# Output blocks summed in accumulating DMA stores, masks by affine selects on GpSimd, and another order

## The chip, the cores and the metric

The kernel runs on one core of a Trainium2 chip. The metric is the device time of one execution in microseconds; the time before is the median of three runs. Engines are called as in the profile: PE (matrix multiplication), DVE (VectorE), ACT (ScalarE), POOL (GpSimd) and SP (SyncE, which here only issues DMAs). Each engine works through its own queue in order; semaphores hold an instruction back until its inputs are there, and everything behind it on that engine waits too.

## What is computed

Causal attention over 8 batches of 8 heads, 576 tokens and 64 columns a head, with 16 further "beacon" keys that every token sees, and behind it a feed-forward layer with an elu between two multiplications (512 to 2048 to 512 columns) on all 4608 tokens.

```python
scores = scale * np.matmul(q, k_all.transpose(0, 1, 3, 2))   # k_all: beacon_k, then k
scores = np.where(causal, -1000000000.0, scores)             # beacons are never masked
a = np.exp(scores - scores.max(-1, keepdims=True))
a /= a.sum(-1, keepdims=True) + 1e-09
x = np.matmul(a, v_all)                    # then (tokens, heads * 64)
h = x @ w_in
g = np.where(h > 0.0, h, np.exp(np.minimum(h, 0.0)) - 1.0)
out = g @ w_out                            # 4608 x 512, float32
```

## The kernel before

The order of all work is written out by hand: one long string of words (L800 to L915) such as `S.3.0` or `J.1.4`, each a step (a function with its arguments) that issues a few instructions. The scheduler keeps that order, so each engine's queue is the string filtered by engine. Letters are steps, the first number a batch (attention) or a tile of tokens (feed-forward).

**Loads.** `lq` (L136), `lv` (L144, L149), `wi` (L160) and `wo` (L163) load queries and keys of the first three batches, values, and the two weight matrices, all by DMAs that POOL issues. From batch 3 on, `lk` (L769) copies q or k of a batch to a scratch in DRAM as bf16, also from POOL, and `lt` (L776) brings it back transposed with DMA transposes issued by SP: `lt.b.0` serves head pairs 0 and 1 (tile qst for one parity of batches), `lt.b.1` pairs 2 and 3. `lp` (L785, L786) puts the beacon keys beside them with small POOL operations.

**Attention.** `T`, `cq`, `ck` transpose q and k of the first batches on PE and drain them. `S` (L318) multiplies scores into one of two PSUM buffers of tag S, `x` (L333, ACT) takes the exponential into the tile et; batches from 1 on have 13 such groups of 512 columns over four head pairs. `m` zeroes what causality forbids by multiplying with triu on DVE (L338): `m.b.p.0` does key blocks 0 and 1 of two head pairs in one operation of 128x1024, `m.b.p.1` blocks 2 and 3 in one and block 4 (80 rows) in another. `D` (L396) adds key blocks on DVE, `L` (L376, L422) sums on PE, `n` (ACT) takes the reciprocal by Ln and Exp, `W` (L376) multiplies by the values, `M` (L474) scales into xT.

**Feed-forward.** Ten tiles of tokens: 0 and 1 have 256, the others 512. `F` (L514) multiplies by w_in, `e` (L524, ACT) takes the exponential, the relu is `u` (L530 on ACT, or with `.v` L532 on DVE) and `k` (L544) makes elu of both on DVE; or `r` (L551) and `g` (L556) make it on DVE without a relu. The last two tiles use a Strassen form with steps X, P, K, E, U (with `.v` on DVE, L737) and V. The second multiplication is in Strassen-Winograd form for all tiles from 1 on (tile 1 takes tile 0 with it): `wt` and `Z` (L566, DVE) make sums of weights and of g, `Q` (L618, PE) runs seven products of 16 matmuls each (words count matmuls, `Q.1.0.7` is the first seven), in PSUM of tag ops with two buffers.

**Output.** After product ph, `J.t.ph` drains it. For ph 0, 2 and 3 the bank is copied to the tile sm on ACT, or on DVE with `.v` (L628). For ph 1, 4 and 5 DVE adds the bank and an sm tile into osb (L635), ph 6 is a copy to osb (L633), and SP stores the 256 KB of osb into its block of the output (L639). sm and osb have three buffers each. The last tile ends with half copies, `Jh`. PE's first words, `wm` and `warm`, are matmuls on zeros.

Of the kernel before, what the change touches and what calls it, by code (L numbers as in the profile page):

```python
# [17 lines left out]
def kernel(  # L18
# [325 lines left out]
    def m(b, p, g):  # L344

        if b > 0:
            t = et4(b, p)
# [273 lines left out]

    @step
    def J(t, ph, eng="s"):

        if ph in (0, 2, 3):
            sm[t, ph] = melt.tile([P, 2, HM], FP32, tag="sm", name="sm")
            for q_, y in both(xy[t, PH[ph][0]]):
                (nc.scalar.copy if eng == "s" else nc.vector.tensor_copy)(out=sm[t, ph][:, q_, :], in_=y)  # L628
# [171 lines left out]
    wm.4 wm.4 warm.4 wm.4 lq.0.0.0.4 lq.0.1.0.4 wm.4 warm.4 ident lq.0.0.4.8 wm.4 T.0.1.0 bt  # L800
    warm.4 lq.0.1.4.8 bk cb.0.3 T.0.0.0 cb.0.1 cb.0.0 ck.0.1.0 S.0.1.0 ck.0.0.0 T.0.1.1 x.0.1.0
    S.0.0.0 x.0.0.0 T.0.0.1 cq.0.1.1 S.0.1.2 cq.0.0.1 T.0.3.0 S.0.0.2 x.0.1.2 T.0.2.0 x.0.0.2
    cq.0.3.0 S.0.0.3 cb.0.2 lq.1.0.0.4 S.0.3.0 T.0.3.1 cq.0.2.0 x.0.0.3 lv.0.0.1 cq.0.3.1
    x.0.3.0 T.0.2.1 S.0.0.1 tri wm.4 x.0.0.1 S.0.3.2 x.0.3.2 S.0.1.3 cq.0.2.1 x.0.1.3 wm.4 wm.4
    S.0.2.0 wm.4 wm.4 x.0.2.0 S.0.3.3 wm.4 x.0.3.3 S.0.2.3 x.0.2.3 wm.4 m.0.3.0 S.0.3.1 cb.1.0
    x.0.3.1 lv.0.2 m.0.1.0 m.0.2.0 m.0.0.0 L.0.A m.0.1.2 n.0.A m.0.0.2 T.1.0.0 wi.2 m.0.3.2
    cq.1.0.0 S.0.2.1 W.0.A.1 x.0.2.1 W.0.A.0 S.0.1.1 x.0.1.1 T.1.1.0 M.0.A.1 S.0.2.2 M.0.A.0
    x.0.2.2 F.0.5 cq.1.1.0 e.0.5 lv.0.3.4 m.0.2.2 wi.1 m.0.0.3 m.0.1.3 S.1.5 S.1.1 x.1.5 m.0.3.3
    F.0.4 x.1.1 lq.1.0.4.8 wi.0 m.0.2.3 L.0.B cb.1.1 e.0.4 W.0.B.1 n.0.B S.1.3 cb.1.3 u.0.4.v
    M.0.B.1 u.0.5.v F.0.2 x.1.3 e.0.2 r.0.2 S.1.4 x.1.4 S.1.0 x.1.0 F.0.3 T.1.3.0 ck.1.3.0  # L810
    W.0.B.0 g.0.2 wi.3 k.0.4 S.1.12 m.1.0.0 k.0.5 M.0.B.0 e.0.3 F.0.1 x.1.12 T.1.2.0 S.1.10
    r.0.3 g.0.3 F.1.0 cq.1.2.0 cb.1.2 e.0.1 u.0.1 x.1.10 k.0.1 F.1.1 e.1.0 S.1.8 lq.2.0.0.4
    u.1.1.v u.1.0 k.1.0 x.1.8 F.0.0 e.1.1 S.1.9 S.1.6 u.0.0.v lq.2.0.4.8 F.0.6 k.1.1 x.1.9
    lp.3.1 e.0.0 T.2.1.0 F.1.3 x.1.6 u.0.6.v e.0.6 cq.2.1.0 S.1.11 cb.2.0 lv.1.0.1 e.1.3 x.1.11
    S.1.7 k.0.0 F.0.7 S.1.2 u.1.3.v F.1.5 x.1.7 x.1.2 T.2.0.0 k.0.6 lv.1.2.3.4 u.0.7.v e.0.7
    m.1.1.1 T.2.2.0 ck.2.0.0 u.1.5.v ck.2.2.0 m.1.1.0 wo.1 e.1.5 m.1.0.1 F.1.6 wo.3 k.0.7 L.1.1
    L.1.0 wo.0 F.1.2 e.1.6 wo.2 k.1.5 lk.3.0 u.1.6.v lk.3.1 F.1.4 cb.2.1 cb.2.2 n.1.1 M.1.1.0
    W.1.0 k.1.6 n.1.0 M.1.0.0 u.1.2 W.1.1 lv.2.2.3.4 u.1.4 M.1.0.1 lk.4.0 e.1.2 lv.3.2.3.4 k.1.3
    S.2.4 e.1.4 x.2.4 F.1.7 M.1.1.1 k.1.4 u.1.7 e.1.7 F.2.13 T.2.3.0 S.2.8 u.2.13 k.1.7 F.2.12
    e.2.13 x.2.8 F.2.9 u.2.12 cq.2.3.0 S.2.3 e.2.12 k.2.13 S.2.1 e.2.9 wt.1.0 k.1.2 x.2.3 F.2.2  # L820
    e.2.2 lv.2.0.1 Z.1.3.B Q.1.0.7 x.2.1 Q.1.7.14 u.2.9.v S.2.2 S.2.0 u.2.2 k.2.12 F.2.6 k.2.9
    Q.1.14.21 x.2.0 x.2.2 F.2.15 cb.2.3 wt.1.1 e.2.6 wt.2.1 u.2.6 u.2.15 Q.1.21.28 e.2.15
    m.2.0.0 S.2.6 S.2.5 wt.2.0 F.2.4 J.1.0 x.2.5 F.2.10 Z.1.1.B Z.1.2.B S.2.11 x.2.6 Q.1.28.35
# [121 lines left out]
```

## Time and profile before

| | |
|---|---|
| median of 3 runs | 330.53 us (330.32 to 330.69) |
| the profiled execution's own time | 329.86 us |
| its span, first to last instruction | 328.2 us |
| granted TensorE clock | 1.0 |
| DMA | 34.65 MB, mean 106 GB/s |
| POOL-issued queue, SP- and ACT-issued queue | 18.49 MB, 15.34 MB |

The profile is of one execution. Its page gives the busy time of each engine, the span in 40 equal slices (a digit is the busy share in tenths), and groups of instructions by line: source line, engine, operation, output and input tiles with shapes, count, then busy time, mean duration in ns, and the idle time of the engine just before them with what ended it. Stretch rows give the busy time of each engine in a part of the span; a timeline lists merged instructions with start and duration. Issues of DMAs have a size and the time from issue to landing.

### The profile page before, as it was taken

Reading aid. Unit: us, or ns where it says so; the run is one execution under the profiler, and the core shown is the slowest. Engines: PE = TensorE matmul, PEld = TensorE weight load, DVE = VectorE, ACT = ScalarE, POOL = GpSimd, SP = SyncE. Lnnn points to the kernel's source line nnn. Section 1 sums busy time; section 2 is a strip of 40 time slices with the busy share of each in tenths; the row PEclk is TensorE's granted clock in tenths of the full one; section 3 lists DMA queues with packets and bytes.
Section 4 is the critical chain, followed back from the end, with each engine's and each line's share of the span. In section 5 each row is a group of like instructions: output and inputs, shape, how many; then the busy total and the mean of one; then the engine's idle time right before and its main releaser. Section 6 shows DMA issues by size and latency. Waiting matters only on the chain.

```text
span 328.2 us, 8827 instructions
## 1 busy us (share of the span) xinstructions
PE 318.5 (97%) x3648; PEld 215.7 (66%) x3648; DVE 296.9 (90%) x527; ACT 276.4 (84%) x449; POOL 85.2 (26%) x109
## 2 busy tenths in 40 slices
PE   7879999999999999999999999999999999999995
PEld 4656766566555655566555665566665888888884
DVE  2677998999998999999989989999999999999992
ACT  2979999998889897999999888988699598889930
POOL 8973791742705626004010500000000000000000
PEclk9999999999999999999999999999999999999999
DMA  9999999999999999995922792010110021111113
GB/s 115 169 190 206 172 167 185 151 151 154 174 173 154 136 172 151 188 116 61 160 82 58 77 106 84 12 34 2 66 34 33 2 96 34 34 65 34 35 64 128
DMA packets 130520, 34.65 MB, mean 106 GB/s; under 512 B 112816, under 2 KB 130480, under 8 KB 130480
## 3 DMA queue, kind: packets, MB, share of 16 engines
q0 software_dynamic: 95840, 18.49, 69.1%
q1 hardware_dynamic: 33920, 15.34, 23.8%
q8 instruction: 28, 0.46, 0.6%
q10 hardware_dynamic: 720, 0.26, 0.3%
q14 instruction: 12, 0.10, 0.1%
HBM read 37.22 MB, written 15.34 MB: 160 GB/s over the span
## 4 chain that ended last, share of the span: by engine, by line
PE 72%; DMA 12%; ACT 7%; POOL 4%; DVE 3%; issue 2%; DVEq 0%; POOLq 0%
PE ops L618 27%; PE hps L514 22%; DMA v<-in_v_dram 10%; PE hps L706 8%; PE sc L318 5%; ACT et L333 5%; PE ut L376 5%; PE sx L618 2%; POOL scr L769 1%; POOL v L149 1%; DMA kst<-in_k_dram 1%; ACT e L524 1%; POOL w_out L163 1%; DVE qkp L396 1%; PE lt L422 1%
## 5 line engine op out<-in xcount | busy, mean ns | idle before, releaser
L333 ACT ACTIVATE et<-sc 128x1024 f16<-128x1024 f32 (+2 forms) x114 | 104.2, 968 | 8.1 <-PE sc L318 7.6
L514 PE MATMUL hps<-xT,w_in 128*128 128x512 f16 (+1 forms) x512 | 110.7, 353 | 0.3 <-DVE gt L556 0.3
L618 PEld LDWEIGHTS <-gt 128*128 128x128 f16 x864 | 83.0, 98 | 21.1 <-issue 2.9
L524 ACT ACTIVATE e<-hps 128x512 f32<-128x512 f32 x112 | 66.7, 615 | 9.0 <-PE hps L514 4.1
L514 PEld LDWEIGHTS <-w_in 128*128 128x128 f16 x512 | 46.8, 98 | 39.0 <-issue 5.5
L544 DVE SCALAR_TENSOR_TENSOR gt<-e,r 128x512 f16<-128x512 f32 x103 | 68.6, 683 | 2.2 <-ACT e L524 0.7
L618 PE MATMUL ops<-w_out,gt 128*128 128x256 f16 x416 | 54.7, 273 | 0.0
L618 PE MATMUL ops<-wt,gt 128*128 128x256 f16 x400 | 53.6, 273 | 0.0
L530 ACT ACTIVATE r<-hps 128x512 f16<-128x512 f32 x74 | 45.0, 616 | 4.5 <-PE hps L514 4.3
L149 POOL DMA_DIRECT2D v<-in_v_dram x40 | 36.4, 1016 | 3.5 <-DMA v<-in_v_dram 1.9
L566 DVE TENSOR_TENSOR gt<-gt 128x2048 f16<-128x2048 f16 (+1 forms) x30 | 33.1, 1110 | 0.1
L338 DVE TENSOR_TENSOR et<-et,triu 128x1024 f16<-128x1024 f16 (+4 forms) x66 | 26.6, 447 | 1.8 <-ACT et L333 1.7
L532 DVE TENSOR_SCALAR r<-hps 128x512 f16<-128x512 f32 x29 | 19.9, 685 | 4.0 <-ACT e L524 3.2
L376 PEld LDWEIGHTS <-v 128*32 128x32 f16 (+1 forms) x800 | 17.2, 96 | 9.4 <-issue 1.2
L745 DVE SCALAR_TENSOR_TENSOR gt<-e,r 128x512 f16<-128x512 f32 x32 | 21.5, 683 | 0.5 <-ACT kst L716 0.4
L376 PE MATMUL ut<-et,v 128*32 128x464 f16 (+3 forms) x560 | 21.1, 296 | 0.3 <-DMA v<-in_v_dram 0.3
L396 DVE TENSOR_TENSOR qkp<-qkp,et 128x1344 f16<-128x1344 f16 (+2 forms) x33 | 19.2, 583 | 0.4
L635 DVE TENSOR_TENSOR osb<-ops,sm 128x512 f32<-128x512 f32 x26 | 17.7, 682 | 1.3 <-PE ops L618 1.3
L716 ACT COPY kst<-hps 128x512 f32<-128x512 f32 x24 | 13.9, 589 | 4.8 <-PE hps L706 4.6
L474 DVE TENSOR_TENSOR xT<-ut,rl 128x672 f16<-128x672 f32 (+12 forms) x26 | 16.4, 669 | 0.7 <-PE ut L376 0.4
L618 PE MATMUL ops<-w_out,s 128*128 128x256 f16 x128 | 16.9, 273 | 0.0
L618 PEld LDWEIGHTS <-s 128*128 128x128 f16 x144 | 13.9, 98 | 2.5
(118 smaller groups left out, 415.7 us busy)
## 6 DMA issues: line engine op xcount, KB each, us to landing
out_dram<-osb SPq DMA_DIRECT2D x35, 256.0 KB, 2.2
v<-in_v_dram POOLq DMA_DIRECT2D x24, 128.0 KB, 11.8
scr<-in_q_dram POOLq DMA_DIRECT2D x5, 576.0 KB, 16.2
scr<-in_k_dram POOLq DMA_DIRECT2D x5, 576.0 KB, 18.1
w_in<-in_moe_w_in_dram POOLq DMA_DIRECT2D x8, 256.0 KB, 8.7
w_out<-in_moe_w_out_dram POOLq DMA_DIRECT2D x4, 512.0 KB, 10.5
qst<-in_q_dram POOLq DMA_DIRECT2D x4, 288.0 KB, 9.6
kst<-in_k_dram POOLq DMA_DIRECT2D x4, 288.0 KB, 10.0
```

The lines of the kernel that those rows point to most:

```text
L149: nc.gpsimd.dma_start(out=vt[b][r0:r0 + n, j, :, :], in_=v[b, :, ilo[j]:ilo[j] + n, :].rearrange("h s d -> s h d"),)
L333: nc.scalar.activation(out=ets[b, d][:, :, a - EC2 * d:e - EC2 * d], in_=sc[b, g][:, :, a - c0:e - c0], func=AFT.Exp, bias=0.0, scale=SCALE)
L338: nc.vector.tensor_tensor(out=o, in0=o, in1=i, op=ALU.mult)
L376: nc.tensor.matmul(out=t[32 * i:32 * (i + 1), a - qa:e - qa], lhsT=ones[0:kc[j], :] if half is None else v16[0:kc[j], j, h, half:D:2], rhs ...
L396: nc.vector.tensor_tensor(out=o, in0=t[0:rows, :, a:e] if n == 0 else o, in1=t[0:rows, :, col:col + e - a], op=ALU.add)
L514: nc.tensor.matmul(out=h[:, n_, :], lhsT=w_in16[:, cc, P * fc:P * (fc + 1)], rhs=xt[k][:, cc, a - TT * k:e - TT * k], start=(cc == 0), sto ...
L524: nc.scalar.activation(out=eb[t, i], in_=flat(hp[t, i]), func=AFT.Exp, bias=0.0, scale=1.0)
L530: nc.scalar.activation(out=rb[t, i], in_=flat(hp[t, i]), func=AFT.Relu, bias=0.0, scale=1.0)
L544: nc.vector.scalar_tensor_tensor(out=half(t, i), in0=eb[t, i], scalar=1.0, in1=rb[t, i], op0=ALU.subtract, op1=ALU.min)
L566: (nc.vector if eng == "v" else nc.gpsimd).tensor_tensor(out=o_, in0=a_, in1=b_, op=op_)
L618: nc.tensor.matmul(out=half_of(xy[t, n_], qd), lhsT=lw[:, P * qd:P * (qd + 1)], rhs=wt_[:, c, :], start=(first and c == 0 and (qd == 0 or ...
L706: nc.tensor.matmul(out=hx[t, g, n_][:, c, :], lhsT=lw, rhs=rh, start=(first and c == 0 and k_ == 0), stop=(k_ == 1), skip_group_check=True)
```

## The change

Three things. First, for all tiles but the last (TA = 9), DVE no longer adds the two parts of an output block. The first part (ph 0, 3 or 2) is stored to its output block from sm by SP as soon as it is drained, the second part (ph 1, 4 or 5) is copied from PSUM to osb by ACT or DVE, and POOL issues a DMA that adds osb to the block in DRAM. Second, 20 of the 40 mask steps go from DVE to POOL (words that end in `.p`): each key block is cut by one affine_select of its own, in place. Third, the whole string is in another order, and some relus, J copies and elu forms are on the other of ACT and DVE. The set of steps is otherwise the same: 1430 words in both.

```diff
+    def cut(o, base):
+        nc.gpsimd.affine_select(
+            out=o, in_=o, compare_op=ALU.is_ge, fill=0.0, base=base, channel_multiplier=-1,
+            pattern=[[0, o.shape[1]], [1, o.shape[2]]])
...
-    def m(b, p, g):
+    def m(b, p, g, eng="v"):
...
+            if eng == "p":
+                for j in (0, 1) if g == 0 else (2, 3, 4):
+                    c, w = lays[b][j][3], min(P, lays[b][j][2] - lays[b][j][1])
+                    cut(t[0:kc[j], :, c:c + w], NB if j == 0 else 0)
+                return
...
+    TA = len(tiles) - 1
+
+    def block(t, ph):
+        i, m_ = {1: (0, 0), 4: (1, 1), 5: (0, 1), 6: (1, 0)}[ph]
+        row = (tiles[t][0] if t > 1 else 0) + 256 * i
+        return out[row:row + 256, HM * m_:HM * (m_ + 1)].rearrange("(q p) m -> p q m", p=P)
...
+            if t < TA:
+                nc.sync.dma_start(out=block(t, {0: 1, 3: 4, 2: 5}[ph]), in_=sm[t, ph])
             return
...
-            if ph == 6:
+            if ph == 6 or t < TA:
...
+        if ph == 6 or t >= TA:
+            nc.sync.dma_start(out=block(t, ph), in_=osb)
+        else:
+            nc.gpsimd.dma_start(out=block(t, ph), in_=osb, accum_op=ALU.add)
```

The queues of POOL and SP that follow from the two strings, from batch 1's values on:

```
POOL before: lq.2.0.4.8 lp.3.1 lv.1.0.1 lv.1.2.3.4 wo.1 wo.3 wo.0 wo.2 lk.3.0 lk.3.1 lv.2.2.3.4
  lk.4.0 lv.3.2.3.4 lv.2.0.1 lp.3.0 lk.4.1 lk.5.1 lk.5.0 lv.3.0.1 lk.6.0 lp.4.1 lp.4.0 lp.5.1 lk.6.1
POOL after:  lq.2.0.0.4 m.1.0.0.p lq.2.0.4.8 lv.1.2.3.4 lv.1.0.1 wo.1 m.1.1.1.p m.1.0.1.p wo.0 wo.2
  wo.3 lp.3.0 lk.3.0 lk.3.1 lv.2.0.1 lk.4.0 lv.2.2.3.4 lk.4.1 m.2.0.0.p J.1.1.v lv.3.2.3.4 lp.4.1
  lp.3.1 lv.3.0.1 m.2.1.0.p J.1.4.v lk.6.1 lp.4.0 J.1.5.v lk.5.0 lk.5.1 m.3.0.0.p lk.6.0 lp.5.0 J.2.1.v
SP before:   lt.3.0 lt.3.1 J.1.1 J.1.4 J.1.5 lt.4.0 J.1.6.v lt.4.1 lt.5.0 J.2.1 lt.5.1 J.2.4
SP after:    lt.3.0 J.1.0.v lt.3.1 J.1.2.v J.1.3 lt.4.0 lt.4.1 J.1.6.v J.2.0.v J.2.2.v lt.5.0 J.2.3
```

More of the change, by code (lines that the diff above doesn't have):

```diff
@@ L799 @@
     run("""
[L800 to L823, printed above, removed]
```

219 lines of the change are left out of this document (122 added, 97 removed).

## The prediction

> **What bounds the kernel now.** I read the busy times first, then the same times by stretch, then the PE's rows with the idle time before each, then the queues that feed PE.
>
> ```profile
> PE 318.5 (97%) x3648; PEld 215.7 (66%) x3648; DVE 296.9 (90%) x527; ACT 276.4 (84%) x449; POOL 85.2 (26%) x109
> ...
> DMA  9999999999999999995922792010110021111113
> ```
> ```profile
> 0.00:10.00 10.00, 8.02 (x96) 4.87 (x96) 3.31 (x13) 3.60 (x5) 8.81 (x18) 1.00 1.05 123
> 10.00:20.00 10.00, 9.31 (x228) 6.66 (x232) 7.27 (x23) 9.93 (x15) 8.84 (x14) 1.00 1.59 176
> 20.00:40.00 20.00, 17.96 (x332) 12.93 (x325) 16.21 (x35) 18.11 (x25) 10.52 (x16) 1.00 1.40 193
> 40.00:60.00 20.00, 19.85 (x348) 12.77 (x346) 18.14 (x34) 19.39 (x32) 10.93 (x12) 1.00 1.69 172
> 60.00:80.00 20.00, 19.96 (x168) 12.37 (x167) 19.72 (x30) 18.78 (x29) 11.43 (x11) 1.00 1.96 149
> 80.00:100.00 20.00, 19.64 (x259) 11.63 (x258) 18.77 (x34) 16.99 (x27) 6.66 (x8) 1.00 2.18 167
> 100.00:120.00 20.00, 19.47 (x200) 11.56 (x197) 18.33 (x30) 18.60 (x28) 10.06 (x11) 1.00 1.75 153
> ...
> 220.00:240.00 20.00, 20.00 (x197) 12.70 (x199) 19.09 (x33) 14.77 (x25) 0.00 (x0) 1.00 0.08 28
> ...
> 320.00:328.20 8.20, 4.58 (x42) 3.84 (x40) 1.97 (x4) 0.37 (x1) 0.00 (x0) 1.00 0.38 128
> ```
>
> The columns of the second fence are the stretch and its length, then PE, PEld, DVE, ACT and POOL, granted clock, DMA share, GB/s. PE is the bound. It is idle 328.2 - 318.5 = 9.7 us in all: 1.98 in the first ten microseconds, 0.69 in the next ten, 2.04 up to 40, 3.62 behind 320 (the last matmul, copy and store), and so only some 1.4 between 40 and 320. From 220 to 240 the idle time is zero although DVE works 19.1 of 20 there. DVE at 90% is thus no second bound: what is taken off it can give back at most those 1.4 us, plus what little it holds up in the start. The second thing to see is that the DMA engines are full until 147 us (the digits are 9 for 18 slices of 8.2 us). Where PE does wait in that time, it waits for a load:
>
> ```profile
> 60.01 1.69 PE L618 MATMUL ops<-w_out,gt 128*128 128x256 f16 x14
> ...
> 78.69 0.63 PE L318 MATMUL sc<-qst 64*128 64x512 bf16 x8
> ...
> 83.00 1.31 PE L376 MATMUL ut<-et,v 128*32 128x464 f16 x36 [0.26 <-DMA v<-in_v_dram]
> ...
> 86.41 0.61 PE L318 MATMUL sc<-kst 64*128 64x272 bf16 x8
> ...
> 104.67 0.61 PE L318 MATMUL sc<-qst 64*128 64x64 bf16 x6 [0.27 <-POOL qst L786]
> ```
>
> So loads arrive just in time at 83.0, and at 104.67 too: the POOL row named there was a write for another batch, and the last thing that batch 4's scores need is its transposed load, which SP issues from 90.7 on. The kernel stands on a full PE fed by a full DMA queue with almost no margin at two places. That is what this change touches.
>
> **The change, part by part.** First the exchange between DVE and ACT.
>
> ```profile
> L544 DVE SCALAR_TENSOR_TENSOR gt<-e,r 128x512 f16<-128x512 f32 x103 | 68.6, 683 | 2.2 <-ACT e L524 0.7 <-PE ops L618 0.7 <-ACT r L530 0.4
> ...
> L532 DVE TENSOR_SCALAR r<-hps 128x512 f16<-128x512 f32 x29 | 19.9, 685 | 4.0 <-ACT e L524 3.2 <-PE hps L514 0.3
> L338 DVE TENSOR_TENSOR et<-et,triu 128x1024 f16<-128x1024 f16 x28 | 18.9, 682 | 0.6 <-ACT et L333 0.5
> L635 DVE TENSOR_TENSOR osb<-ops,sm 128x512 f32<-128x512 f32 x26 | 17.7, 682 | 1.3 <-PE ops L618 1.3
> ...
> L556 DVE TENSOR_TENSOR gt<-hps,r 128x512 f16<-128x512 f32 x9 | 6.2, 691 | 0.3
> L628 DVE COPY sm<-ops 128x512 f32<-128x512 f32 x7 | 4.8, 681 | 0.0
> ...
> L551 DVE TENSOR_SCALAR r<-e 128x512 f16<-128x512 f32 x9 | 4.5, 497 | 1.5 <-ACT e L524 1.5
> L338 DVE TENSOR_TENSOR et<-et,triu 80x320 f16<-80x320 f16 x14 | 4.4, 315 | 0.0
> ...
> L737 DVE TENSOR_SCALAR r<-kst 128x512 f16<-128x512 f32 x3 | 1.3, 421 | 0.0
> ```
>
> An addition (L635) costs DVE 682 ns and the copy that takes its place 681 (L628), so a block left on DVE saves nothing; only those that go to ACT do. By the order's words DVE has 24 J steps in place of 37: 13 x 0.682 = 8.9 us off. Masks: 12 steps with one 128x1024 operation (batch 0's one, which is smaller, counted so) and 8 with a 128x1024 and an 80x320 one, 12 x 0.682 + 8 x 0.997 = 16.2 off. Added: 10 more relus of a tile (L532), 6.9, and 7 of the last two tiles (L737), 2.9. Three elu blocks change from the r,g form to the k form: 3 x (0.683 - 0.497 - 0.691) = -1.5. DVE: -16.8 us. ACT takes 13 copies and gives 14 relus: about nothing. PE's work is the same, matmul for matmul. With the 1.4 us of the first part, I put this relief at -0.5 (0 to -1.4).
>
> Next the masks on POOL and what stands behind them.
>
> ```profile
> L238 POOL TENSOR_SCALAR_AFFINE_SELECT triu<-triu 128x256 f16<-128x256 f16 x1 | 0.4, 402 | 0.0
> ...
> L238 POOL TENSOR_SCALAR_AFFINE_SELECT triu<-triu 128x128 f16<-128x128 f16 x1 | 0.3, 287 | 0.1
> ```
> ```profile
> 40.05 3.02 POOL L163 DMA_DIRECT2D w_out<-in_moe_w_out_dram  x4
> 43.00 2.31 POOL L769 DMA_DIRECT2D scr<-in_q_dram  x1
> ```
> ```profile
> 42.59 2.85 ACT L333 ACTIVATE et<-sc 128x1024 f16<-128x1024 f32 x3
> ```
> ```profile
> 59.27 6.10 SPq L776 DMA_TRANSPOSE qst<-scr  x2
> 65.48 7.61 SPq L776 DMA_TRANSPOSE kst<-scr  x2
> ```
>
> From 256 and 128 columns, 0.9 ns a column: a cut of 4x128 is estimated at 0.63 us, one of 4x80 at 0.46. The 20 masks are 49 cuts, about 28.7 us of POOL, which has room (85 of 328). It is their place that costs. In the new order two masks of batch 1 stand in POOL's queue ahead of three of the four w_out loads and of batch 3's scratch copies. The second needs x.1.2, the last of the three ACT operations that end at 45.4. Before, POOL issued these loads from 40 to 47 waiting for nobody. Now the mask runs 45.4 to 47.2 at best, 49 if it waits for its turn beside DVE, and the loads behind it go 6 to 8 us later. Three w_out pieces of 512 KB at the stretch's 172 GB/s are 3.0 us each, so the last lands at 56 to 59, and the first reader on PE is at 60.0: just covered. The two scratch copies land by the same rate some 7 us later, at 64 to 67 in place of 59.3 (where SP's transposes begin). SP then needs 6.1 and 7.6 us for them, and the second pair now has tile 1's first output store ahead of it. Their readers on PE are at 78.7 and 86.4; before, with 9.2 us from an issue to its landing (row below), the first pair was down by 62.3 + 9.2 = 71.5 and the second by some 78.5, 7 and 8 us ahead of them. That margin is used up. I take 1.0 us for this, between 0 and 4.
>
> The third part is the traffic of the accumulating stores.
>
> ```profile
> out_dram<-osb SPq DMA_DIRECT2D x2, 256.0 KB, 7.7
> ```
> ```profile
> out_dram<-osb SPq DMA_DIRECT2D x35, 256.0 KB, 2.2
> ...
> qst<-scr SPq DMA_TRANSPOSE x10, 9.2
> ```
>
> The first row is from 115 to 123 us: a store lands 7.7 us after its issue while the loads run, 2.2 over the whole kernel. Each of eight tiles now has three more transfers, 24 x 256 KB, and three of its seven read the output back to add. Tiles 1 and 2 and the start of 3 fall in the full stretch: 14 more transfers by 150 us, 6 of them by 105. At 153 to 172 GB/s 256 KB are 1.5 to 1.7 us; an accumulating one isn't shown by any row, so between the same and twice that. Six are 9 to 15 us of DMA time, less if stores fill gaps of the small packets, ahead of the load that PE met with 0.27 us of waiting at 104.67. Against it: SP's new order puts batch 4's transposes ahead of J.1.5's and J.1.6's stores, where they stood behind J.1.5 and so started at 90.7. That gives back up to about 10 us. Also, POOL's accumulating stores wait in their queue for the first store to land, and behind J.1.1 stand batch 3's values and the beacon columns, behind J.1.5 batch 5's copies. I take 1.0 us, between 0 and 6. Behind that stretch I let the same transfers cost nothing: the digits fall to 0 to 2 with a few loads between, POOL has little else to do, and a store lands in 2.2 again.
>
> Then the lock, where the trace shows one side only:
>
> ```profile
> 130.29 0.72 POOL L786 COPY qst<-bkT 128x32 bf16<-128x32 bf16 x1
> ...
> 143.66 0.21 POOL L786 COPY qst<-bkT 128x32 bf16<-128x32 bf16 x1 [12.65 <-PE sc L318]
> ```
> ```profile
> 130.26 0.93 DVE L338 TENSOR_TENSOR et<-et,triu 128x1024 f16<-128x1024 f16 x2
> ...
> 143.62 0.68 DVE L635 TENSOR_TENSOR osb<-ops,sm 128x512 f32<-128x512 f32 x1
> ```
>
> The same small POOL copy takes 0.21 beside a DVE operation that reads PSUM and SBUF, and 0.72 beside one that reads SBUF twice: it ends only when the first mask has. So a cut on POOL will wait for DVE's k, Z, D and mask operations, 0.5 us or so each time. Whether DVE also waits for a cut, no row shows, since POOL's copies are too short. The loss on DVE is between nothing and 28.7 us, the whole time of the cuts; if two thirds of DVE's time are such operations (an estimate: k in L544 alone is 68.6 of 296.9, and Z, D and the masks come on top), about 19. The relief is 16.8, so DVE ends between 280 and 309, and I count 0.5 us for PE (0 to 5), near the middle where both cancel.
>
> The Trainium skill, SBUF — State Buffer, section "Who interferes with whom", says that a DVE instruction with two SBUF inputs and a GpSimd instruction that reads SBUF exclude each other, and that the second one waits for all of the first. The trace agrees for the POOL side (0.21 against 0.72); by that rule the DVE side is the 19 us above.
>
> The start: the warm-up matmuls are as many, and 16 score blocks pass through ACT, which is busy 9.93 of 10 us from 10 to 20, in either order. 0, with 1.5 either way. The tail is the same copies and stores: 0.
>
> Sum: -0.5 + 1.0 + 1.0 + 0.5 + 0 = +2.0 us on the profiled execution's 329.86 (span 328.2 and 1.66 around it), 331.9; the median of the runs lies 0.67 above that execution, so 332.5. The case by itself spans 331.3 to 335.
>
> **Rivals.** (1) Faster: PE's holes close. The waits at 83.0 (batch 2's values now go ahead of batch 3's), 104.67 and those of the start, 4.7 us up to 40, shrink, and a DVE with 17 us less work holds nobody up. For it: these waits are real, and SP's order does let batch 4's load go earlier. Against it: most of the start waits for first loads and for ACT, which the change doesn't shorten. Price -0.7 to -2.5; at -1.3, 329.2. It decides if the scratch copies of batch 3 land before 64 us and no two-input DVE operation is longer than its 0.68. (2) Everything is absorbed: 330.5, within 0.2%, about what a measurement of this kernel can tell from no change. For it: 8 us of margin on the transposes, and no PE idle at all after 120. (3) The lock bites: DVE waits for nearly every cut, D and k come late, PSUM banks are not freed, and PE stalls from 90 to 235 us, where the masks are. Of the 19 to 29 us that DVE loses, what goes beyond the 16.8 taken off it, 2 to 12, reaches PE by half: 1 to 6, with the late loads' 2 it is +3 to +8, 336. For it: the 0.72 row and a DVE at 19.7 of 20. Against: the 16.8 us taken off DVE. (4) POOL's queue blocks so hard (each wait of an accumulating store delays loads behind it) that a batch's loads are late by more than 5 us: over 337.
>
> **How the numbers follow.** Forecast 0.40 (332.5), rival 1 0.27, rival 2 0.13, rival 3 0.14, rival 4 0.06. Faster by over 0.2% (0.66 us): 0.27. Within: 0.13. Slower: 0.40 + 0.14 + 0.06 = 0.60. The range leaves out rival 4 and the far end of rival 1 and of rival 3: 329.0 to 337.5.
>
> **What would show it.** Right: PE idle of 1 to 3 us between 55 and 130, before sc<-qst, sc<-kst, ut or ops rows, with a DMA as releaser; w_out issued after 47; SP's first transposes after 64; stores in the full stretch landing after more than 7 us. Lock: L544, L566 and L396 rows above their 683 to 1220 ns while POOL cuts, and cuts of 1 us and more. Wrong: PE idle before 40 us below 4.7 and none between 40 and 130 (rival 1), or PE waiting for DVE after 150 us, where I see no cost at all.

## The result: 343.6 us, 4% slower

The changed kernel takes 343.60 us (343.27 to 345.92), the kernel before 330.42 us on the same chip: a ratio of 1.0415, 95% interval 1.0367 to 1.0462. That is 13.2 us more, where I forecast 2.0, and far beyond the range's end at 337.5. The profiled execution took 343.88 us with a span of 342.2.

Page of the changed kernel, busy times and DMA slices:

```profile
PE 321.4 (94%) x3647; PEld 216.9 (63%) x3648; DVE 296.2 (87%) x498; ACT 277.3 (81%) x448; POOL 152.9 (45%) x182
...
DMA  9999979999999999999991328913213352352362
```

Two things are to be seen. DVE is as busy as before (296.2 against 296.9), although by the words of the order 16.8 us of work went from it. And PE is idle for 342.2 - 321.4 = 20.8 us in place of 9.7, and 2.9 us longer busy with the same matmuls; together 14.0, the growth of the span. The same stretches as before show where (length, PE, PEld, DVE, ACT, POOL, granted clock, DMA share, GB/s):

```profile
20.00:40.00 20.00, 17.75 (x354) 13.03 (x342) 14.83 (x32) 16.86 (x23) 11.23 (x17) 1.00 1.31 186
40.00:60.00 20.00, 18.60 (x341) 12.55 (x338) 18.44 (x31) 18.16 (x29) 14.57 (x18) 1.00 1.21 141
60.00:80.00 20.00, 19.61 (x164) 11.69 (x163) 19.94 (x28) 18.90 (x31) 10.33 (x9) 1.00 2.05 164
80.00:100.00 20.00, 20.00 (x262) 12.18 (x260) 18.80 (x35) 17.48 (x26) 13.00 (x20) 1.00 1.91 169
100.00:120.00 20.00, 15.25 (x126) 8.50 (x123) 13.41 (x17) 15.19 (x22) 14.38 (x18) 1.00 1.98 177
120.00:140.00 20.00, 16.26 (x196) 8.96 (x197) 15.91 (x26) 13.90 (x23) 8.08 (x9) 0.83 2.08 157
```

From 40 to 60 PE is idle for 1.40 us (before 0.15), from 100 to 140 for 8.49 (before, 0.53 from 100 to 120). Two rows of PE carry most of that, and both wait for DVE (start, duration, what, and in brackets the idle time before it with its releaser):

```profile
49.42 0.90 PE L390 MATMUL lt<-et,ones 128*32 128x464 f16 x24 [1.18 <-DVE et L338]
...
123.74 0.58 PE L436 MATMUL lt<-qkp,ones 128*32 128x464 f16 x4 [7.89 <-DVE qkp L410]
```

What DVE was doing at these two times:

```profile
45.44 3.05 DVE L558 SCALAR_TENSOR_TENSOR gt<-e,r 128x512 f16<-128x512 f32 x2
...
116.46 4.22 DVE L410 TENSOR_TENSOR qkp<-qkp,et 128x1344 f16<-128x1344 f16 x2 [4.78 <-POOL et L341]
```

and POOL:

```profile
33.02 1.26 POOL L341 TENSOR_SCALAR_AFFINE_SELECT et<-et 128x512 f16<-128x512 f16 x2 [5.67 <-ACT et L333]
...
44.68 4.15 POOL L341 TENSOR_SCALAR_AFFINE_SELECT et<-et 128x512 f16<-128x512 f16 x6 [3.40 <-issue]
48.78 2.25 POOL L163 DMA_DIRECT2D w_out<-in_moe_w_out_dram  x3
...
113.61 7.54 POOL L341 TENSOR_SCALAR_AFFINE_SELECT et<-et 128x512 f16<-128x512 f16 x10
```

Two k operations took 3.05 us (683 ns each before), with six cuts beside them. Two D operations took 4.22, with cuts beside them, after DVE had waited 4.78 for POOL; in e17 below, with no cuts there, the same two take 1.47:

```profile
111.80 1.47 DVE L410 TENSOR_TENSOR qkp<-qkp,et 128x1344 f16<-128x1344 f16 x2
```

The grouped rows say how general this is on DVE (count, busy time, mean ns), first D's of the kernel before, then those of the changed one:

```profile
L396 DVE TENSOR_TENSOR qkp<-et 128x1856 f16<-128x1856 f16 x11 | 12.3, 1115 | 0.1
L396 DVE TENSOR_TENSOR qkp<-qkp,et 128x1344 f16<-128x1344 f16 x11 | 9.3, 848 | 0.1
```

```profile
L558 DVE SCALAR_TENSOR_TENSOR gt<-e,r 128x512 f16<-128x512 f32 x106 | 75.8, 729 | 4.1 <-ACT r L544 2.8 <-ACT e L538 1.0
L410 DVE TENSOR_TENSOR qkp<-et 128x1856 f16<-128x1856 f16 x11 | 14.3, 1298 | 0.1
L410 DVE TENSOR_TENSOR qkp<-qkp,et 128x1344 f16<-128x1344 f16 x11 | 11.6, 1055 | 4.8 <-POOL et L341 4.8
L341 POOL TENSOR_SCALAR_AFFINE_SELECT et<-et 128x512 f16<-128x512 f16 x38 | 40.5, 1429 | 22.8 <-ACT et L333 19.4 <-issue 3.4
```

k went from 683 to 729, D from 1115 and 848 to 1298 and 1055. The mean of 1429 for a cut is not what a cut costs POOL, since the records of neighbouring cuts overlap (38 of them would make 54.3 us, and the busy time is 40.5). The ten cuts at 113.61 take 7.54 us together, 0.75 each, and the six at 44.68 take 4.15, 0.69 each, where the two at 33.02 took 0.63 each. So POOL loses a little, and DVE much more.

Third, the chain of work that ended last, followed through the large hole (start, length, what):

```profile
94.38 0.81 POOL out_dram L663
95.19 2.68 POOL scr L792
...
99.67 4.47 POOL scr L792 x2
104.14 1.24 POOL et L341 x2
105.38 5.61 issue
...
114.60 1.84 POOL et L341 x3
...
116.46 2.89 DVE qkp L410
...
123.74 0.58 PE lt L436 x4
```

It lies in POOL's queue: accumulating store, scratch copies, cuts, 5.6 us of waiting at the next copy, more cuts, and then DVE and PE. Two fine stretches complete the picture, one of the DMA engines, one of the clock:

```profile
46.00:48.00 2.00, 2.00 (x58) 1.78 (x56) 2.00 (x2) 2.00 (x4) 2.00 (x4) 1.00 0.23 38
48.00:50.00 2.00, 0.82 (x19) 0.37 (x20) 2.00 (x4) 0.93 (x1) 2.00 (x3) 1.00 0.00 0
...
124.00:126.00 2.00, 2.00 (x40) 1.14 (x36) 0.97 (x2) 1.32 (x3) 1.89 (x3) 0.50 1.59 182
126.00:128.00 2.00, 2.00 (x23) 0.81 (x16) 1.16 (x3) 0.98 (x3) 0.00 (x0) 0.50 1.65 131
```

While POOL cuts ahead of the w_out loads the DMA engines run empty, in a stretch in which they had been full; and behind the hole PE works at half its clock for some four microseconds.

### The profile page after: what moved, and what is told of

The parts are those of the page before. It is cut to its first block, busy times and chain, and to the rows that moved or that the text cites. A ratio compares the mean times of both kernels' runs of the same rounds, so it can differ in the third digit from the quotient of the medians.

```text
span 342.2 us, 8938 instructions
## 1 busy us (share of the span) xinstructions
PE 321.4 (94%) x3647; PEld 216.9 (63%) x3648; DVE 296.2 (87%) x498; ACT 277.3 (81%) x448; POOL 152.9 (45%) x182
## 4 chain that ended last, share of the span: by engine, by line
PE 53%; DVE 23%; ACT 9%; issue 8%; POOL 5%; DMA 2%; DVEq 0%; ACTq 0%; POOLq 0%
PE ops L632 20%; PE hps L528 13%; PE hps L729 7%; DVE gt L558 6%; DVE qkp L410 5%; ACT et L333 4%; PE sc L318 4%; PE ut L390 3%; DVE xT L488 3%; POOL scr L792 2%; DVE r L546 2%; PE sx L632 2%; ACT e L538 2%; DVE gt L580 2%; DMA kst<-in_k_dram 2%
## 5 line engine op out<-in xcount | busy, mean ns | idle before, releaser
L528 PE MATMUL hps<-xT,w_in 128*128 128x512 f16 (+1 forms) x512 | 112.0, 354 | 1.1 <-DVE r L546 0.6
L663 POOL DMA_DIRECT2D out_dram<-osb x24 | 31.7, 1322 | 133.3 <-DVE osb L656 47.4
L558 DVE SCALAR_TENSOR_TENSOR gt<-e,r 128x512 f16<-128x512 f32 x106 | 75.8, 729 | 4.1 <-ACT r L544 2.8
L341 POOL TENSOR_SCALAR_AFFINE_SELECT et<-et 128x512 f16<-128x512 f16 (+4 forms) x49 | 45.8, 1342 | 22.8 <-ACT et L333 19.4
L544 ACT ACTIVATE r<-hps 128x512 f16<-128x512 f32 x67 | 40.5, 613 | 6.6 <-PE hps L528 5.0
L149 POOL DMA_DIRECT2D v<-in_v_dram x40 | 38.4, 1245 | 1.7 <-issue 1.7
L546 DVE TENSOR_SCALAR r<-hps 128x512 f16<-128x512 f32 x39 | 26.7, 684 | 4.8 <-ACT e L538 4.3
L410 DVE TENSOR_TENSOR qkp<-qkp,et 128x1344 f16<-128x1344 f16 (+2 forms) x33 | 23.5, 711 | 5.6 <-POOL et L341 4.8
L390 PEld LDWEIGHTS <-v 128*32 128x32 f16 (+1 forms) x800 | 18.3, 100 | 9.2 <-issue 1.9
L768 DVE SCALAR_TENSOR_TENSOR gt<-e,r 128x512 f16<-128x512 f32 x32 | 21.3, 682 | 0.1
L792 POOL DMA_DIRECT2D scr<-in_q_dram x5 | 12.9, 2574 | 11.4 <-PE sc L318 5.6
```

Source lines behind the costliest of these rows:

```text
L149: nc.gpsimd.dma_start(out=vt[b][r0:r0 + n, j, :, :], in_=v[b, :, ilo[j]:ilo[j] + n, :].rearrange("h s d -> s h d"),)
L341: nc.gpsimd.affine_select(out=o, in_=o, compare_op=ALU.is_ge, fill=0.0, base=base, channel_multiplier=-1, pattern=[[0, o.shape[1]], [1, o. ...
L390: nc.tensor.matmul(out=t[32 * i:32 * (i + 1), a - qa:e - qa], lhsT=ones[0:kc[j], :] if half is None else v16[0:kc[j], j, h, half:D:2], rhs ...
L410: nc.vector.tensor_tensor(out=o, in0=t[0:rows, :, a:e] if n == 0 else o, in1=t[0:rows, :, col:col + e - a], op=ALU.add)
L528: nc.tensor.matmul(out=h[:, n_, :], lhsT=w_in16[:, cc, P * fc:P * (fc + 1)], rhs=xt[k][:, cc, a - TT * k:e - TT * k], start=(cc == 0), sto ...
L544: nc.scalar.activation(out=rb[t, i], in_=flat(hp[t, i]), func=AFT.Relu, bias=0.0, scale=1.0)
```

## The experiments

Three theories, which the expectations name. **Queue**: in POOL's single queue masks and accumulating stores hold up the loads behind them, and loads hold up masks. **Lock**: DVE's operations with two SBUF inputs and POOL's cuts wait for each other, and DVE is late where PE needs it. **Traffic**: the additional stores slow the loads. Some runs name a **latency** theory as well: masks on POOL are simply later. All results, each beside the kernel before on the same chip, DVE's busy time from the profiled execution. The ratio and its interval are estimated from all runs and need not be the quotient of the two medians; a cost in us is the difference of the medians.

| run | us | before | ratio (95% interval) | DVE busy |
|---|---|---|---|---|
| changed kernel | 343.60 | 330.42 | 1.0415 (1.0367 to 1.0462) | 296.2 |
| e1 masks on DVE | 336.97 | 330.56 | 1.0197 (1.0129 to 1.0264) | 298.0 |
| e2 additions on DVE | 345.06 | 330.56 | 1.0420 (1.0364 to 1.0476) | 303.3 |
| e3 copy behind masks | 343.13 | 330.56 | 1.0369 (1.0306 to 1.0432) | 301.8 |
| e4 order alone | 345.76 | 330.56 | 1.0447 (1.0401 to 1.0493) | 305.6 |
| e5 accumulating stores alone | 334.30 | 330.43 | 1.0109 (1.0064 to 1.0154) | 284.3 |
| e6 masks alone | 337.58 | 330.43 | 1.0228 (1.0154 to 1.0302) | 293.0 |
| e7 fillers | 344.13 | 330.43 | 1.0394 (1.0335 to 1.0452) | 299.7 |
| e8 late masks | 330.82 | 330.66 | 1.0003 (0.9978 to 1.0027) | 295.5 |
| e9 early masks | 335.51 | 330.66 | 1.0136 (1.0078 to 1.0194) | 293.8 |
| e10 late accumulating stores | 331.40 | 330.66 | 1.0023 (0.9995 to 1.0051) | 288.8 |
| e11 idle cuts | 336.37 | 330.66 | 1.0143 (1.0081 to 1.0204) | 303.3 |
| e12 idle memsets | 331.29 | 331.07 | 0.9991 (0.9962 to 1.0020) | 296.9 |
| e13 masks from batch 2 on | 333.45 | 331.07 | 1.0055 (1.0028 to 1.0082) | 295.9 |
| e14 transposes first | 334.08 | 331.07 | 1.0078 (1.0046 to 1.0111) | 284.4 |
| e15 first masks back | 340.85 | 331.07 | 1.0281 (1.0212 to 1.0349) | 298.6 |
| e16 loads ahead | 344.04 | 330.89 | 1.0383 (1.0333 to 1.0433) | 301.4 |
| e17 late masks only | 336.13 | 330.89 | 1.0164 (1.0118 to 1.0209) | 296.4 |

### Undoing one part, in either order (e1, e2, e4, e5, e6)

e1 is the changed kernel with its 20 masks on DVE again:

```diff
- m.1.0.0.p   (and 19 more words with .p)
+ m.1.0.0
```

> The changed kernel with its 20 masks back on DVE; accumulating stores and order stay. Queue theory (batch 3's masks stand on POOL behind a scratch copy that waits 5.6 us, DVE and PE wait for them): the 7.9 us hole before L436 goes, and with it the slow clock behind it; 332 to 335. Lock theory (DVE waits for POOL's cuts throughout): the same hole goes and DVE's k rows are 683 again; 331 to 334. Traffic theory (the extra DMA transfers delay loads): hardly better, 340 or more, with PE waiting for loads.

e2 is the changed kernel with the additions on DVE and plain stores:

```diff
-    TA = len(tiles) - 1
+    TA = 0
```

> The changed kernel with all additions on DVE and plain stores; masks on POOL and order stay. Queue theory, if it is the accumulating stores' own waits on POOL that push three scratch copies together: copies go out earlier, the hole goes, 332 to 336. Lock theory: the cuts still cost DVE some 13 us, to which 9 come back: 338 to 344. Traffic theory: 331 to 333.

e4 has both of these edits, and so only the new order. 

> The changed kernel's order and its choice of engines for relus and copies, with additions and masks on DVE as before. If the order costs nothing by itself: 330 to 332, with DVE the fuller by 16 us of masks. If the order alone puts loads late: 334 or more, with PE waiting between 40 and 60 us.

e5 is the kernel before with the changed `J` and its stores, in its own order:

```diff
+    TA = len(tiles) - 1
...
+            nc.gpsimd.dma_start(out=block(t, ph), in_=osb, accum_op=ALU.add)
```

> The kernel before, in its own order, with the accumulating stores alone; nearly all second copies are then on ACT. Queue theory: POOL's queue waits for stores, but no mask stands behind them: 331 to 334, loads later by up to 10 us. Traffic theory: 335 or more, PE waiting for loads between 80 and 130. Lock theory: 330 to 331.

e6 is the kernel before with `cut` and the same 20 masks on POOL:

```diff
- m.1.0.0
+ m.1.0.0.p   (and 19 more)
```

> The kernel before, in its own order, with the 20 masks on POOL alone. Lock theory: cuts of 1.2 to 1.4 us, k rows above 700 ns, D rows above 1150, and 334 to 340. Queue theory: it depends on what stands ahead of the masks on POOL; batch 3's copies are spaced in this order, so 331 to 336 with shorter holes than 7.9. Traffic theory: 330.

Measured: in the order of before, accumulating stores cost 3.9 us and the masks 7.2; taken off the changed kernel the masks give back 6.6. What neither explains is the order: e1 (order and accumulating stores) is at +6.4, 2.5 over e5. Alone the order costs 15.2 us, and then DVE is at 305.6, 8.7 over before; with accumulating stores it is at 298.0. PE's idle time from 180 to 240 us is 3.29 us in e4, 3.11 in e2, 1.74 in e1 and 0.63 in the changed kernel, most of it in e4 and e2 in rows that name DVE. So the order needs a lighter DVE; putting the additions back into the changed kernel moves nothing that can be told (e2). The parts are thus not independent: in the new order, the masks on POOL cost 6.6 us with accumulating stores (e1 to the changed kernel) and nothing without them (345.76 in e4, 345.06 in e2). Stores and masks together in the old order were not run. DVE's busy time shows what the masks did for it, page lines of e1 and e6:

```profile
PE 320.5 (96%) x3647; PEld 216.8 (65%) x3648; DVE 298.0 (89%) x528; ACT 277.2 (83%) x448; POOL 116.2 (35%) x133
```
```profile
PE 320.6 (95%) x3648; PEld 216.2 (64%) x3648; DVE 293.0 (87%) x497; ACT 276.7 (82%) x449; POOL 127.8 (38%) x158
```

Moving 16.2 us of masks off DVE lightened it by 298.0 - 296.2 = 1.8 us in the new order and by 296.9 - 293.0 = 3.9 in the old one. The rest came back as longer operations. That is what the lock theory says of DVE; whether it is also the cause of the time is left to the next runs.

### The hole at 116 us (e3, e7)

e3 moves the scratch copy that waits 5.6 us ahead of batch 3's masks behind them:

```diff
- m.3.0.0.p ... lk.6.0 ... m.3.1.1.p
+ m.3.0.0.p ... m.3.1.1.p lk.6.0
```

> The changed kernel with one word moved: batch 6's scratch copy of q stands on POOL behind batch 3's masks in place of ahead of them. Queue theory: the hole of 7.9 us and the 2 us of half clock behind it go, 333 to 336. Lock theory: the cuts are as long, 341 to 344. Traffic theory: 343.

The time stayed (343.13), and so did the hole, a little smaller:

```profile
125.18 0.58 PE L436 MATMUL lt<-qkp,ones 128*32 128x464 f16 x4 [6.41 <-DVE qkp L410]
```

The copy alone is not the cause. In e1, without any mask on POOL, the same row waits too, but for less:

```profile
117.10 0.38 PE L436 MATMUL lt<-qkp,ones 128*32 128x464 f16 x4 [2.15 <-DVE qkp L410]
```

The new order asks for this sum when DVE still has work ahead of it. With the masks and the accumulating stores on POOL the wait grows from 2.15 to 7.89; with the same masks and no accumulating store, in e2, it is no longer than in e1:

```profile
118.19 0.38 PE L436 MATMUL lt<-qkp,ones 128*32 128x464 f16 x4 [2.34 <-DVE qkp L410]
```

So the long hole comes of both together in POOL's one queue, as e2's first expectation had it. But the time did not follow: PE's idle time from 100 to 140 us is 8.49 us in the changed kernel and 3.40 in e2, and e2, with a fuller DVE, loses as much elsewhere. e7 fills the hole with matmuls whose result is overwritten, extra work:

```diff
+            for _ in range(34 if (b, g) == (3, 0) else 0):
+                nc.tensor.matmul(
+                    out=t[:, 0:512], lhsT=w_in16[:, 0, 0:P], rhs=w_in16[:, 0, 0:512], start=True, stop=True,
+                    skip_group_check=True)
```

> The changed kernel with 34 idle matmuls of 512 columns (7.3 us) on PE ahead of batch 3's first sums, in the hole; they write a bank that is overwritten. If the clock of 0.5 behind the hole costs time of its own: 341 to 342, some 2 us less. If only the hole counts: 343 to 344.

```profile
120.00:140.00 20.00, 20.00 (x233) 11.44 (x232) 16.06 (x26) 15.89 (x27) 8.34 (x8) 1.00 2.13 156
```

The clock stayed at 1.00 and no idle time is left there, yet the median is 344.13. The profiled execution was the fastest of four (341.68), so 2 us for the half clock can't be excluded; the median doesn't show them. PE has to wait for DVE there, busy or not.

### Which masks, and why (e8, e9, e13, e11, e12)

Three runs of the kernel before with part of e6's masks on POOL: batches 4 to 7 (10 masks), batches 0 to 3 (10), and batches 2 to 7 (16).

```diff
- m.4.0.0
+ m.4.0.0.p   (e8: batches 4 to 7; e9: 0 to 3; e13: 2 to 7)
```

> The kernel before with the 10 mask steps of batches 4 to 7 on POOL, nothing else. Twenty masks in this order cost +7.1 us. Queue theory (the price is the delay of the loads that stand behind the masks in POOL's queue): by then POOL has few loads left, so 330.4 to 331.2. Lock theory (the price is DVE's lengthened operations): half the cuts, half the price, 333.5 to 334.5, with k rows (L544) over 700 ns behind 150 us and PE idle there. Latency theory (D and the sums wait for cuts that are slower than DVE's one operation): 331 to 333, with PE idle before lt rows behind 150 us.

> The kernel before with the 10 mask steps of batches 0 to 3 on POOL. Queue theory: nearly the whole price of the 20, 336 to 338, with w_out and the scratch copies issued 3 to 9 us later as with all 20. Lock theory: half, 333.5 to 334.5. Latency theory: some 332 to 334, with idle time before lt rows rather than before rows that read loaded tiles.

> The kernel before with 16 masks on POOL; the four of batches 0 and 1 (m.0.1.0, m.1.0.0, m.1.1.1, m.1.0.1) stay on DVE, so that no mask stands ahead of batch 2's loads, of w_out and of batch 3's copies. All 20 cost 7.1, the 10 of batches 4 to 7 cost 0.2, the 10 of batches 0 to 3 cost 4.9. Queue theory: the four first ones hold the loads (POOL waits 9.3 us for ACT ahead of batch 2's keys and the DMA engines run empty at 32 to 37 us), so 330.5 to 332. Lock or latency theory: 16 of 20 parts, 335 to 336.5.

Late masks cost nothing and bring nothing; early ones 4.9 us; without the first four, e6's 1.0228 falls to 1.0055, so these four are worth some 5 us. (Early and late ones by themselves make 5.0 of the 7.2; e6's interval, 5.1 to 10, is too wide to say whether the rest is real.) In e9 one of them, m.1.0.0, stands ahead of batch 2's loads. Its row of POOL and its fine stretch:

```profile
33.61 1.61 POOL L341 TENSOR_SCALAR_AFFINE_SELECT et<-et 128x512 f16<-128x512 f16 x2 [9.31 <-ACT et L333]
```
```profile
34.00:36.00 2.00, 2.00 (x50) 1.52 (x38) 1.24 (x4) 1.81 (x3) 2.00 (x4) 1.00 0.00 0
```

POOL waits 9.3 us for an exponential, the loads behind it wait too, and the DMA engines are empty in a stretch that is full in the kernel before (202 GB/s from 34 to 36). In e6 it is the same (a wait of 9.15 us, 3 GB/s from 34 to 36), and its longest wait on PE shows who pays:

```profile
88.07 0.38 PE L390 MATMUL lt<-et,v 128*32 128x112 f16 x8 [3.93 <-DMA v<-in_v_dram]
```

PE waits 3.93 us for batch 2's values, which are late: in the kernel before, PE waited 0.26 us for them, at 83.00. In e9 the same row waits 2.25. POOL issued batch 3's scratch copies at 51.6 in place of 43.0, and the values stand in its queue behind those and the copies that follow. In e13, where the first four masks are on DVE, the copies go out at 43.5, and this row doesn't wait. This is the queue with its victim: of the 5.7 us that PE is idle longer in e6 than before (15.4 against 9.7), 3.6 lie from 80 to 100 us, around this row. The longest of e6's other waits behind 40 us (1.10 before a sum at 49.18) and of those that e13 keeps (1.34 and 1.19 from 80 to 90 us) name DVE. e11 and e12 take up the lock. e11 is the kernel before, masks on DVE, with 46 cuts of up to 384 columns more on POOL at the words of 19 masks, on a tile that nobody reads; e12 has memsets in their place. The output is complete in both; this is extra work.

```diff
+    dm = konst.tile([P, 4, 96], FP16, name="dm")
...
+                    cut(dm[0:kc[j], :, 0:w], 0)                     # e11
+                    nc.gpsimd.memset(dm[0:kc[j], :, 0:w], 0.0)      # e12
```

> The kernel before with its masks on DVE, and 46 further cuts on POOL at the words of 19 masks, on a tile of their own that nobody reads; the output is complete, the cuts are extra work. Nobody waits for them. Latency theory: 330.4 to 331 (nothing waits). Queue theory: the cuts of batches 1 and 2 hold POOL's loads up by their own 4 to 8 us without waiting for ACT, 331 to 334. Lock theory: DVE is as loaded as before and stretched by up to 46 x 0.6 = 28 us, part of it beside operations that read PSUM: 334 to 340, with DVE's busy time above 300.

> The idle cuts again, each replaced by a memset of the same tile at the same word: POOL is held up in the same places, but reads no SBUF. The output is complete, the memsets are extra work. The idle cuts cost 5.7 us, with DVE busy 303.3. Lock theory: the memsets leave DVE at 296 to 297.5 and cost 0 to 1 us, 330.5 to 331.7. Queue theory (POOL's loads later by the time the instructions in front take): 333 to 336 with DVE unchanged.

Idle cuts cost 5.7 us, idle memsets at the same words nothing. e11's group rows, then e12's:

```profile
L341 POOL TENSOR_SCALAR_AFFINE_SELECT dm<-dm 128x384 f16<-128x384 f16 x38 | 32.2, 848 | 1.7
...
L557 DVE SCALAR_TENSOR_TENSOR gt<-e,r 128x512 f16<-128x512 f32 x103 | 71.0, 707 | 1.9 <-PE ops L631 0.7 <-ACT e L537 0.6 <-ACT r L543 0.4
```
```profile
L359 POOL MEMSET dm<- 128x384 f16 x38 | 17.9, 472 | 1.4
...
L557 DVE SCALAR_TENSOR_TENSOR gt<-e,r 128x512 f16<-128x512 f32 x103 | 68.7, 684 | 2.2 <-ACT e L537 0.9 <-PE ops L631 0.7 <-ACT r L543 0.5
```

Beside cuts k takes 707 ns and DVE is busy for 303.3 us; beside memsets, 684 and 296.9, as before. In these runs POOL's memsets, which only write SBUF, leave DVE alone, and its cuts, which read it, don't; and since nobody waits for these cuts the latency theory can't explain the loss. The Trainium skill, SBUF — State Buffer, section "Who interferes with whom", says the same: a DVE instruction with two SBUF inputs contends with a GpSimd instruction that reads SBUF, "not with one that only writes it". These runs agree (707 against 684). Some reservations: POOL also spends longer on the cuts than on the memsets, so e11's loads behind them go later (the last three of w_out at 46.5, in e12 at 43.6; PE then waits 0.86 us for values at 85.47, 0.24 in e12), and e11's profiled execution had a clock of 0.50 at 24 to 26 us; the one execution of e11 with a mean clock of 1.0 took 334.25. Not all of the 5.7 need be the lock. And e12 says nothing against the queue: its memsets wait for no exponential, and the DMA engines stay full (202 GB/s from 34 to 36).

### The first loads in the new order (e15, e16, e17)

e15 is the changed kernel with the first four masks on DVE; e17 has all masks of batches 0 to 3 there. e16 keeps all 20 on POOL and moves the loads instead:

```diff
- m.1.0.0.p lq.2.0.4.8 lv.1.2.3.4 lv.1.0.1 wo.1 m.1.1.1.p m.1.0.1.p wo.0 wo.2 wo.3 lp.3.0 lk.3.0 lk.3.1
+ lq.2.0.4.8 lv.1.2.3.4 lv.1.0.1 wo.1 m.1.0.0.p wo.0 wo.2 wo.3 lk.3.0 lk.3.1 m.1.1.1.p m.1.0.1.p lp.3.0
```

> The changed kernel with the four masks of batches 0 and 1 back on DVE, 16 still on POOL. The changed kernel takes 343.6, with all 20 on DVE 337.0. Queue theory: nearly all of it comes back, 337 to 339. Lock or latency theory (the hole of 7.9 us ahead of L.3.0 is made by batch 3's masks): 341.5 to 343.5, with that hole still there.

> The changed kernel, all 20 masks on POOL, with the loads that stood behind batch 1's masks in POOL's queue moved ahead of them: batch 2's second half of q and k, batch 1's values and one piece of w_out ahead of m.1.0.0, the other three pieces of w_out and batch 3's copies ahead of m.1.1.1. No work changes its engine. The changed kernel takes 343.6; with these four masks on DVE it takes 340.9. Queue theory: the same gain or more, 339.5 to 341.5, and no stretch without DMA traffic at 46 to 50 us. Lock theory: the gain came from fewer cuts, so 343 to 344.5.

> The changed kernel with the 10 masks of batches 0 to 3 on DVE and the 10 of batches 4 to 7 on POOL. The changed kernel takes 343.6, with the first four back on DVE 340.9, with all 20 back 337.0. If batch 3's masks, which wait in a row behind a scratch copy and leave PE idle for 3.9 us with the clock at 0.85 behind it, make the rest of the loss: 336.5 to 338, without that hole. If each cut costs the same by the lock: half of 6.6 remains, 340 to 340.5.

e15 lies between (1.0281), e17 (1.0164) is not to be told from e1, which has no mask on POOL at all. So here too the early ten cost everything and the late ten nothing. e16 was the test between queue and lock, and the queue theory's forecast failed: the DMA engines had no hole any more, and the time stayed at 344.04. Its stretch, and its rows of POOL, DVE and PE:

```profile
48.00:50.00 2.00, 0.49 (x12) 0.31 (x16) 2.00 (x3) 0.10 (x1) 2.00 (x6) 1.00 1.23 208
```
```profile
47.17 4.87 POOL L341 TENSOR_SCALAR_AFFINE_SELECT et<-et 128x512 f16<-128x512 f16 x6
```
```profile
46.50 2.95 DVE L338 TENSOR_TENSOR et<-et,triu 128x1024 f16<-128x1024 f16 x1
```
```profile
49.51 1.17 PE L390 MATMUL lt<-et,ones 128*32 128x464 f16 x24 [2.10 <-DVE et L338]
```

One mask on DVE, 0.68 us before, takes 2.95 beside the cuts, and PE waits 2.1 us for exactly this mask. That is the lock with its victim. But e16 is not a clean test. Its six cuts now stand behind the loads and start at 47.17, 2.5 us later than in the changed kernel; behind the wait the granted clock is 0.50 from 52 to 54 us. The hole ahead of L.3.0 shrinks to 3.72 us, and PE's idle time as a whole from 20.8 to 18.7, but PE is busy for 324.6 us in place of 321.4. So e16 shows that moving these loads doesn't pay, and not that their delay costs nothing. The same two k operations that took 3.05 in the changed kernel take 1.28 in e15, where the cuts are gone:

```profile
45.59 1.28 DVE L558 SCALAR_TENSOR_TENSOR gt<-e,r 128x512 f16<-128x512 f32 x2
```

### The accumulating stores (e10, e14)

e10 is e5 with the additions of tiles 1 to 3 on DVE, so that 15 of 24 accumulating stores are left, all behind 150 us. e14 is e5 with SP's transposes of batch 3 ahead of the first store.

```diff
-            if ph == 6 or t < TA:
+            if ph == 6 or TB <= t < TA:        # e10, TB = 4
...
- J.1.0 ... lt.3.0 lp.3.0 lt.3.1
+ lt.3.0 lt.3.1 J.1.0 ... lp.3.0               # e14
```

> The kernel before with accumulating stores for tiles 4 to 8 alone (15 of the 24); tiles 1 to 3 are added on DVE. All 24 cost +3.8 us. Traffic theory and queue theory: the stores of tiles 4 to 8 fall behind 150 us where the DMA engines are nearly free and POOL issues few loads, so 330.0 to 330.8, and DVE is some 10 us lighter for nothing. Lock theory or another price for each accumulating store: 15 of 24 parts of 3.8, so 332.5 to 333.

> The kernel before with accumulating stores alone, and SP's transposes of batch 3 (lt.3.0, lt.3.1) moved ahead of the first output store of tile 1 (J.1.0) in the order. With accumulating stores alone it was 334.3, and SP issued these transposes at 67.7 in place of 59.3, behind that store, which waits for its copy until 67.1. SP-queue theory: most of the 3.8 us goes, 331 to 332.3. Traffic theory: the additional bytes remain, 333.5 to 334.5.

The late 15 cost 0.7 us, with an interval that takes in zero (-0.2 to 1.7), so some 3 of e5's 3.9 belong to tiles 1 to 3, in the stretch where DMA is full. e5's longest wait on PE behind the start is for scores of batch 3, which need these transposes:

```profile
81.01 0.63 PE L318 MATMUL sc<-qst 64*128 64x512 bf16 x8 [1.87 <-issue]
```

In e14 the transposes start at 61.1 and not at 67.7, and this wait is gone; the time is 1.0078 against 1.0109. The intervals overlap, so what SP's queue costs is not shown, and most of the loss stays without it. What remains is their traffic, or their waits in POOL's queue. e5's row for the second one:

```profile
89.98 1.19 POOL L649 DMA_DIRECT2D out_dram<-osb  x1 [13.10 <-ACT r L530]
```

Batch 5's copies stand behind that. I have not separated the two.

## Why the prediction was wrong, point by point

- **PE is the bound, and a lighter DVE gives nothing.** Right in the old order: e10 took 8.1 us off DVE (288.8) where DMA and POOL are nearly free, and was no faster. In the new order it does not hold: e1 has 7.6 us less on DVE than e4 and is 8.8 us faster.
- **DVE's sum, -16.8.** Right as counted: e4, with masks and additions back on DVE, has 305.6, so the relus and elu forms added 8.7, where I had 6.9 + 2.9 - 1.5 = 8.3.
- **The lock, +0.5 (0 to 5).** This is the step that failed. Its size on DVE was about right: I put DVE's loss near 19 us, and the masks' 16.2 came back but for 1.8 (14.4 lost; 12.3 in the old order). Its price on PE was wrong. I set loss against relief over the whole span, "near the middle where both cancel". They do not lie in the same place: the relief of the late masks buys nothing (e8, 1.0003), and the early cuts fall at 44.7 to 48.8 and 101 to 121 us, where PE's next row needs DVE. The two rows at 49.42 and 123.74, 9.1 us of waiting, are most of the 11.1 us that PE is idle longer than before, and both wait for DVE: two k operations that took 3.05 us in place of 1.28, and two D operations that first waited 4.78 for the cuts and then took 4.22 in place of 1.47. Lock and queue together, which I had at 1.5 us, cost 6.6 to 7.2.
- **Masks in POOL's queue, +1.0 (0 to 4).** The rows came out as forecast: the last w_out pieces issued from 48.8 and SP's first transposes at 64.7 (I had 47 to 49, and after 64). Their consequence did not: I expected PE to wait 1 to 3 us for loads between 55 and 130, and from 60 to 100 us PE is idle for 0.39 us, as before (0.40). What I had not seen is the other direction: the mask's reader waits for POOL (the 4.78 above), and POOL waits at a scratch copy (5.6 us) or an accumulating store ahead of the mask. I priced who waits behind a mask in POOL's queue and never who waits for the mask. In the old order, which I did not forecast, the wait behind the masks is the larger part (3.93 us for the values in e6).
- **Traffic, +1.0 (0 to 6).** Inside its bounds, which were wide, at 3.9, and in the place named: tiles 1 to 3. That it is the traffic, and not the waits in POOL's or SP's queue, is not shown. No row gives the DMA time of one accumulating store, which I had put between the same as a plain one's and twice that; the times to landing stand at 4.4 us to 3.6 and 2.5 for the two kinds of plain store:

```profile
out_dram<-sm SPq DMA_DIRECT2D x24, 256.0 KB, 3.6
out_dram<-osb POOLq DMA_DIRECT2D x24, 256.0 KB, 4.4
...
out_dram<-osb SPq DMA_DIRECT2D x11, 256.0 KB, 2.5
```

- **The order.** I gave it no term but its queues, and no reason for that. e1 less e5 says 2.5 us, in the wait of 2.15 ahead of L.3.0 among others; alone it costs 15.2.
- **The start, 0, and the tail, 0.** From 20 to 40 us PE is busy 17.75 in place of 17.96, and behind 320 us it is idle for 3.99 in place of 3.62; no loss that matters.
- **The rivals.** The third had the price of the masks and half of their mechanism (+3 to +8, "from 90 to 235 us"; nearly all of it lay ahead of 128), the fourth the queue. I gave them 0.14 and 0.06 as if each stood alone. They came together: 3.9 for the stores, then 2.5 for the order, then 6.6 for the masks are the 13.2 us but for the difference between chips. That they add up is no test, since each is what its step added to the one before; in another sequence the same parts have other prices (order alone 15.2, masks on top of it nothing). The upper ends of my own three bounds (4, 6 and 5) add up to 15, and the range stopped 7 us above the median, as if no two of them could come together.

What stays open: how the price of the early masks divides between lock and queue. Both have a victim on PE: the queue in e6 (3.93 us for late values) and, the other way round, in D's wait of 4.78 for POOL; the lock in e16 (a mask of 2.95 us that PE waits for) and in e11. In the old order the first four masks, which hold the loads, are worth some 5 of 7.2 us, and 2.4 remain without them (e13). In the new order no run has cuts without the lock. No version tried beats the kernel before; the nearest, e8 and e12, equal it.

## What to carry to other kernels

Work moved between two engines that hold each other up is not taken away: count what comes back, and compare loss and relief stretch by stretch, at the rows for which the bound engine waits, not over the span. On an engine that also issues the loads, ask of each new instruction both who stands behind it and who waits for its result. Where an engine's queue and the DMA are full up to some time and free behind it, make such a change only behind that time: there it cost nothing, but with nobody waiting there it brought nothing either. And don't add up what single parts cost when the order of work changes too: the price of one part depended on the others.

## What the hardware showed that I had not expected

- A train of cuts goes on while a DVE operation waits. The ten cuts at 113.61 took 0.75 us each and the six at 44.68 took 0.69, against 0.63 without a DVE operation for most of their time; beside them two D operations took 4.22 us in place of 1.47 and two k operations 3.05 in place of 1.28, and in e16 a DVE mask of 0.68 took 2.95. Both sides lose, DVE by far the most.
- Issuing an accumulating store holds POOL for some 1.2 us (1.19 in e5's row), against 0.75 for a piece of w_out (2.25 for three, above). The wait ahead of it, 13.10 us in that row, is longer by far, and the loads behind it wait too.
- After the hole of 7.9 us the granted clock was 0.50 until 128 us. The Trainium skill, TensorE: Matmul & The Clock Gate, section "What's actually happening", has the clock halved after an idle window of about 3.4 us; the trace agrees with that order of time: PE has nothing to do from 115.9 on, and the clock is 1.00 up to 120 and 0.81 in the mean from 120 to 122. But in e9 and e11 the clock fell to 0.50 at 24 to 26 us as well, with 1.35 to 1.6 us of idle time of PE at 20 to 24, and in e16 at 52 to 54 behind a wait of 2.10, while the changed kernel, with 1.9 us idle at 20 to 24, kept 1.00 there. Why, no run here shows.
